# Turning logit spectra on chip with VectorE block transpositions, and a new order for the hand-over to the experts

## The chip, the cores and the metric

One Trainium2 chip (trn2), one core. The metric is device time in microseconds of one execution, the median of several. The profile and the trace are of one execution on that core. PE is the matrix engine (TensorE), PEld its weight loads, DVE is VectorE, ACT is ScalarE, POOL is GpSimd, SP only issues DMAs.

## The reference, cut to what matters

```python
X = np.fft.rfft(x, axis=1)                       # x: 8 batches x 3072 x 256
Yr = Xr @ w_r - Xi @ w_i + b_r;  Yi = Xr @ w_i + Xi @ w_r + b_i
Y  = soft_threshold(Yr, 0.01) + 1j * soft_threshold(Yi, 0.01)
x  = np.fft.irfft(Y, n=3072, axis=1).reshape(24576, 256)
logits = x @ phi                                  # 32 slots
d = softmax(logits, over tokens);  slot_input = d.T @ x
slot_out[e] = relu(slot_input[e] @ w1[e]) @ w2[e] # 8 experts, 4 slots each, 1024 wide
c = softmax(logits, over slots);   x = c @ slot_out
out = mish(x @ w_in) @ w_out                      # 2048 wide
```

All arrays are float32. The token softmax runs over all 24576 tokens, so nothing of the experts can start before the last batch's logits have been weighed.

## The kernel before, in words

The transform of length 3072 is done as 128 x 24. For each batch `stage1` multiplies by the 128-point matrix `f1`, the result goes to memory and comes back with the frequencies in other places (`load_b`), and for each of 32 blocks (four per batch, eight frequency pairs each) `stage2` multiplies by twiddled 24-point matrices. `xh` and `xl` are the rounded value and its rest: for each of six PSUM tiles of a block ACT copies `xh` (L230) and DVE subtracts `xl` (L231), one pair after the other. `linear` is the complex product, in groups of six matmuls `l` (three groups for each half of the features, here called a, b and c by their weights), followed on DVE and ACT by `k`, `p`, `cl` and on POOL by `yt`. `ytrans` transposes `yt` to `y` for the slot sums.

The logits need no inverse transform of the 256 features: `project` (`pp`) applies phi to the spectrum first, giving 32 slots, DVE transposes that (`phat`), `inv1` (`iu`) does the 24-point part of the inverse, and `inv2` (`lps`) the 128-point part for a whole batch. Between `inv1` and `inv2` the axes have to be exchanged. Before, `inv1` transposes 32x32 blocks on DVE into `u` (L295), stores them to the memory tensor `udr` in four pieces per block (L300), and `c_load` reads the batch back as `v` (L314). Then come the maximum over tokens (`smax1`: `rm`; `smax2`: `mt`, `mb`), the exponential `dx` (`smax3`), the softmax over slots (`csoft1`, `csoft2`, `ctrans`, stored to `c_d`), the forward transform of the weights `dx` (`fwd1`: `dps`, copied to `dm`, stored to `ddr` and read back as `dd` by `d_load`; `fwd2`: `dt`; `dturn`: `tn`), the slot sums with `y` (`slots`: `sps`) and the weight sums (`dsum`, `dsum2`: `rd`, `dsp`). A running maximum rescales sums of earlier batches.

The order of the work on every engine is that in which the pieces are issued: each piece is put in a list with a position (`at`), block k at about k, and the list is sorted. The table `PA` gives offsets for all batches and `TAIL` the positions for the last ones; there `NK` is 32, the number of blocks. Engines run their own instructions in that order, and SP its DMAs. `warm` issues small products that nothing reads.

After the last block comes the hand-over: the remaining `y`, the last batch's logits, weights and slot sums, the weight sum, and `sip`, which makes the slot inputs `sit`. Then the experts (`hp`, `htp`, `so`, `sop`), the mixed matrix `mp`, and the FFN over 24576 tokens (`h`, `g`, `o`, from L785), which fills the rest. Expert weights are loaded into room that the loop's pools leave (`right.close`, position "rc"; tiles `w1t` and `w2t`), and, once `sit` is made and the left pools are closed, `raw` (three more `w2`), `win`, `ctt` and `wof`.

Of the kernel before, what the change touches and what calls it, by code (L numbers as in the profile page):

```python
# [24 lines left out]
FF = 2048  # L25
LAM = 0.01
TINY2 = float(np.array([897 << 20], np.int32).view(np.float32)[0].astype(np.float64) ** 2)


def constants():  # L30
# [38 lines left out]
def body(ctx, tc, x, w_r, w_i, b_r, b_i, phi, w1, w2, w_in, w_out, cbig, ct, out, dbg=None, stop=False):  # L69
# [53 lines left out]
    x_t, b_t, xh_t, xl_t, yt_t, y_t, pt_t, k1_t = {}, {}, {}, {}, {}, {}, {}, {}  # L123
    sdr, udr, ddr, ch, a_t = {}, {}, {}, {}, {}
    XC = 512
# [185 lines left out]

    def c_load(b):
        v = cp.tile([128, N2, NS], F32, tag="v", name="v")
        nc.sync.dma_start(out=v, in_=udr[b].rearrange("q (r n) s -> (q r) n s", r=4))  # L314
        ch[b] = v

    def inv2(b):
        v = ch[b]
        lg = cp.tile([128, 6, 4, NS], F32, tag="lg", name="lg")
        for i in range(2):  # L320
            ps = psum([128, 12, NS], "lps")
            nc.tensor.matmul(ps, lhsT=f1t, rhs=v[:, 12 * i:12 * i + 12], start=True, stop=True)
            nc.scalar.activation(out=lg[:, :, 2 * i:2 * i + 2].rearrange("p i j s -> p j i s"), in_=ps.rearrange("p (j i) s -> p j i s", j=2),
                                 func=AF.Copy, scale=1.0 / 1536.0)
        ch[b] = lg

    def smax1(b):
        lg = ch[b]
        rm = sm.tile([128, 2, NS], F32, tag="rm", bufs=1, name="rm")
        for i in range(2):  # L330
            nc.vector.tensor_reduce(rm[:, i], lg[:, :, 2 * i:2 * i + 2].rearrange("p i j s -> p s i j"), axis=AX.XY, op=ALU.max)
        rm4 = sm.tile([128, 4, NS], F32, tag="rm4", name="rm4")
        nc.vector.tensor_max(rm4, rm[:, None, 0].to_broadcast([128, 4, NS]), rm[:, None, 1].to_broadcast([128, 4, NS]))
        ch[b, 4] = rm4

    def smax2(b):
# [18 lines left out]
    def smax3(b):  # L355
        lg = ch[b]
        ps = psum([128, NS], "mb")
        nc.tensor.matmul(ps, lhsT=ones32, rhs=ch[b, 2], start=True, stop=True)
        dx = cp.tile([128, N2, NS], F32, tag="dd", name="dx")
        nc.vector.tensor_sub(dx.rearrange("p (j i) s -> p j i s", j=4), lg.rearrange("p i j s -> p j i s"),  # L360
                             ps[:, None, None, :].to_broadcast([128, 4, 6, NS]))
        nc.scalar.activation(out=dx, in_=dx, func=AF.Exp)
        ch[b, 1] = dx
# [31 lines left out]
    def fwd1(b):  # L395
        d = ch[b, 1]
        dm = cp.tile([128, N2, NS], F32, tag="v", name="dm")
        for i in range(2):
            ps = psum([128, 12, NS], "dps")
            nc.tensor.matmul(ps, lhsT=f1, rhs=d[:, 12 * i:12 * i + 12], start=True, stop=True)  # L400
            nc.scalar.activation(out=dm[:, 12 * i:12 * i + 12], in_=ps, func=AF.Copy)
        ddr[b] = dram.tile([NP, 96, NS], F32, tag="ddr", bufs=2, name="ddr")
        (nc.scalar if b == NB - 1 else nc.sync).dma_start(out=ddr[b].rearrange("q (r n) s -> (q r) n s", r=4), in_=dm)

    def d_load(b):
        dd = cp.tile([96, NP, NS], F32, tag="dd", name="dd")
        nc.sync.dma_start(out=dd, in_=ddr[b].rearrange("q p s -> p q s"))
        ch[b, 0] = dd

# [8 lines left out]
    def dsum2(b):  # L418
# [4 lines left out]
        else:  # L423
            ab = ab_t[b]
            nc.vector.tensor_scalar(d_acc, d_acc, ab[:, 0:1], None, op0=ALU.mult)
            nc.vector.scalar_tensor_tensor(d_acc, ps, ab[:, 1:2], d_acc, op0=ALU.mult, op1=ALU.add)

    def fwd2(b, g):
        dd = ch[b, 0]
        ps = psum([128, 2, 96], "dt")  # L430
        for i in range(2):
            for j in range(4):
                q = 8 * g + 2 * j + i
                nc.tensor.matmul(ps[32 * j:32 * j + 32, i], lhsT=dd[:, q, :], rhs=t_m[:, q, 0:96],
                                 start=True, stop=True, tile_position=(0, 32 * j))
        dt = cp.tile([128, 2, 96], F32, tag="pt", bufs=2, name="dtt")
        nc.scalar.activation(out=dt, in_=ps, func=AF.Copy)
        ch[b, 7, g] = dt

    def dturn(b, g):  # L440
# [4 lines left out]
        t = cp.tile([96, 2, 128], F32, tag="dh", bufs=4, name="dh")  # L445
        nc.scalar.activation(out=t, in_=ps, func=AF.Copy)
        ch[b, 5, g] = t
# [35 lines left out]
    def conv(srcd, dstd, i, step):  # L483
# [5 lines left out]
        if step == 1:  # L489
            src = cv["n"]  # L490
            cv.update(lo=src[:, :, 0].bitcast(U32), hi=src[:, :, 1])
            for t in "abc":
                cv[t] = cvp.tile([128, n], I32, tag="c" + t, name="cv" + t)
        lo, hi, a, b, c = (cv[t] for t in ("lo", "hi", "a", "b", "c"))
        if step == 1:
# [53 lines left out]
    for b in range(NB):  # L549
        f2 = pos("f2", b)  # L550
        for n, f in (("cl", c_load), ("i2", inv2), ("m1", smax1), ("m2", smax2), ("m3", smax3), ("f1", fwd1), ("c1", csoft1),
                     ("ds", dsum), ("dl", d_load), ("c2", csoft2), ("ds2", dsum2)):
            at(pos(n, b), f, b)
        for g in range(4):
            at(f2 + 0.1 * g, fwd2, b, g)
            at(f2 + 0.1 * g + 0.15, dturn, b, g)
        if b < NB - 1:
            at(pos("sl", b), slots, b)
        else:
            for g in range(4):  # L560
                at(f2 + 0.1 * g + 0.27, slots, b, (g,))
        for g in range(2):
# [85 lines left out]
class Experts:  # L648
# [37 lines left out]
    def run(self, big, psh, pso, sit, ident, sot, load_rest):  # L686
# [39 lines left out]
        for g in range(2):  # L726
# [3 lines left out]
            for h in range(2):  # L730
# [4 lines left out]

PA = dict(y=20, s1=-5.89, s1d=0.3402, lb=-1.91, s2=-1.1, s2d=0.0002, pj=1.18, yt=2.24, ytd=0.0002, cl=0.78, i2=1.17, m1=1.17, m2=1.34, m3=1.51, f1=1.84, c1=1.58, ds=1.76, dl=2.05, c2=2.57, ds2=8.73, f2=2.46, sl=3.2, rc=0.3, cx=3.24, cxd=0.0002, x0=-0.79, x1=0.05, ytl=1.05, x2=1.3, x3=2.7)


TAIL = {
# [7 lines left out]
    "warm": ((0.83, 7), (1.175, 5), (1.3, 2), (1.395, 3), (1.76, 20), (2.32, 15), (3.5, 4)),  # L747
}
# [134 lines left out]
```

## Time and profile before

| | us |
|---|---|
| median of 3 runs | 1995.45 |
| lowest, highest | 1987.47, 1995.67 |
| profiled execution: span from the first to the last instruction | 1995.2 |
| PE busy in the span | 1942.3 (97%) |
| DVE, ACT, POOL busy | 1169.1, 903.3, 195.1 |
| chain that ended last: PE, ACT, DVE | 80%, 9%, 6% |

The profiled execution's own time is not listed apart from its span; the span lies 0.25 us below the median. Busy time of PE is from matmuls that overlap, so it is read together with the idle notes of its rows: a wait is written as [us of idle <- what ended it]. A share over the whole span mixes three stages (loop, hand-over, FFN), so the rows below are by stretch.

### The profile page before, as it was taken

The numbers are of one execution on the slowest core, as the hardware profiler recorded it, in microseconds if no ns is written. First come the engines' busy times: TensorE is split into PE (matmuls) and PEld (weight loads), VectorE is DVE, ScalarE is ACT, GpSimd is POOL, SyncE is SP. The second block draws the span as 40 slices with busy tenths as digits, with TensorE's granted clock in tenths as the row PEclk, the third lists the DMA queues.
The fourth block names the chain that finished last, engine by engine and source line by source line (L and its number), as shares of the span: only waits on it lengthen the run. The fifth ranks groups of instructions, "written<-read, shape, count | busy, mean of one in ns | idle before, by whom it ended". The sixth has DMA issues, their size and how long they took to land.

```text
span 1995.2 us, 30611 instructions
## 1 busy us (share of the span) xinstructions
PE 1942.3 (97%) x12344; PEld 1623.3 (81%) x12344; DVE 1169.1 (59%) x1767; ACT 903.3 (45%) x1479; POOL 195.1 (10%) x245
## 2 busy tenths in 40 slices
PE   7899999999998999999999999999999999999999
PEld 5677787777877768888888888888888888888887
DVE  3345545556455547666666666666666666666665
ACT  2666666667665433333333333333333333333332
POOL 0332332332323100000000000000000000000000
PEclk9999998999999899999999999999999999999999
DMA  8755665566643690002002002002002002000000
GB/s 248 233 151 173 167 185 141 170 173 160 184 142 78 213 297 27 20 13 53 22 22 53 22 22 53 22 22 53 11 22 53 22 22 53 22 22 22 22 22 22
DMA packets 131150, 171.39 MB, mean 86 GB/s; under 512 B 57136, under 2 KB 96688, under 8 KB 130752
## 3 DMA queue, kind: packets, MB, share of 16 engines
q1 hardware_dynamic: 128512, 164.10, 28.0%
q0 software_dynamic: 1792, 4.76, 0.8%
q8 instruction: 97, 1.59, 0.3%
q10 hardware_dynamic: 704, 0.57, 0.1%
q14 instruction: 45, 0.37, 0.1%
HBM read 102.29 MB, written 67.11 MB: 85 GB/s over the span
## 4 chain that ended last, share of the span: by engine, by line
PE 80%; ACT 9%; DVE 6%; issue 2%; POOL 1%; DMA 1%; ACTq 0%; SPq 0%; DVEq 0%; POOLq 0%
PE o L815 54%; PE h L785 9%; PE l L250 5%; DVE xl L231 3%; PE s L222 3%; ACT xh L230 2%; PE s L193 2%; ACT cl L268 2%; ACT p L269 2%; PE sps L457 1%; ACT y L309 1%; PE tr L307 1%; POOL yt L270 1%; DVE p L262 1%; PE pp L281 1%
## 5 line engine op out<-in xcount | busy, mean ns | idle before, releaser
L815 PE MATMUL o<-whl,gh 128*128 128x512 f32 x3072 | 1082.9, 395 | 0.0
L815 PE MATMUL o<-whl,gl 128*128 128x256 f32 x3072 | 827.8, 280 | 0.0
L791 ACT ACTIVATE g<-h 128x1024 f32<-128x1024 f32 x384 | 394.3, 1027 | 746.3 <-PE h L785 733.6
L815 PEld LDWEIGHTS o<-whl,gh 128*128 128x128 f32 x3072 | 566.5, 188 | 121.5
L815 PEld LDWEIGHTS o<-whl,gl 128*128 128x128 f32 x3072 | 578.5, 188 | 31.5
L800 DVE TENSOR_TENSOR gl<-g,gh 128x1024 fp32r<-128x1024 f32 x384 | 470.2, 1224 | 28.9 <-DVE gh L796 0.9
L796 DVE CAST gh<-g 128x1024 fp32r<-128x1024 f32 x384 | 265.8, 692 | 351.1 <-ACT g L791 351.0
L785 PE MATMUL h<-ctt,mst 128*128 128x512 f32 x768 | 240.8, 395 | 0.0
L231 DVE TENSOR_TENSOR xl<-s,xh 128x432 fp32r<-128x432 f32 (+1 forms) x192 | 106.1, 558 | 153.1 <-ACT xh L230 153.1
L270 POOL TENSOR_TENSOR yt<-cl,p 128x384 f32<-128x384 f32 x124 | 126.2, 1017 | 435.1 <-ACT p L269 309.6
L222 PE MATMUL s<-tall,bt 96*128 96x144 f32 x1024 | 137.0, 294 | 8.9 <-DMA bt<-sdr 4.5
L222 PEld LDWEIGHTS s<-tall,bt 96*128 96x128 f32 x1024 | 134.9, 197 | 13.0 <-issue 12.0
L230 ACT ACTIVATE xh<-s 128x432 fp32r<-128x432 f32 (+1 forms) x192 | 90.8, 490 | 114.0 <-DVE xl L231 77.4
L785 PEld LDWEIGHTS h<-ctt,mst 128*128 128x128 f32 x768 | 121.2, 188 | 17.9 <-DVE mst L772 0.5
L262 DVE TENSOR_TENSOR p<-l,k 128x384 f32<-128x384 f32 x128 | 70.6, 553 | 91.3 <-PE l L250 58.9
L823 DVE TENSOR_TENSOR os<-o,os 128x256 f32<-128x256 f32 x192 | 76.6, 419 | 77.4 <-ACT os L822 77.4
L268 ACT ACTIVATE cl<-p,tup 128x384 f32<-128x384 f32 x124 | 76.3, 615 | 91.6 <-DVE p L262 71.4
L193 PE MATMUL s<-xc,cb 128*128 128x512 f32 x192 | 103.8, 632 | 7.8 <-DMA xc<-in_x_dram 7.8
L822 ACT ACTIVATE os<-o 128x256 f32<-128x256 f32 x192 | 73.7, 384 | 41.6 <-PE o L815 37.7
L269 ACT ACTIVATE p<-p,tlo 128x384 f32<-128x384 f32 x124 | 76.4, 616 | 4.0
L309 ACT ACTIVATE y<-tr 96x512 f32<-96x512 f32 x128 | 66.1, 592 | 14.6 <-PE tr L307 14.6
L307 PEld LDWEIGHTS tr<-cb,yt 128*96 128x96 f32 x512 | 54.0, 126 | 18.9 <-DVE xl L231 7.0
(176 smaller groups left out, 1539.7 us busy)
## 6 DMA issues: line engine op xcount, KB each, us to landing
bt<-sdr SPq DMA_DIRECT2D x32, 768.0 KB, 8.2
out_dram<-os SPq DMA_DIRECT2D x47, 512.0 KB, 2.6
xc<-in_x_dram SPq DMA_DIRECT2D x42, 512.0 KB, 5.2
sdr<-a SPq DMA_DIRECT2D x42, 512.0 KB, 3.2
ctt<-c_d SPq DMA_DIRECT2D x28, 384.0 KB, 7.1
c_d<-chl SPq DMA_DIRECT2D x16, 384.0 KB, 3.1
w1t<-in_moe_w_dram SPq DMA_DIRECT2D x6, 1024.0 KB, 6.9
w2t<-in_moe_w_dram SPq DMA_DIRECT2D x5, 1024.0 KB, 11.0
```

The costliest lines, as they stand in the source:

```text
L193: nc.tensor.matmul(ps, lhsT=f1, rhs=xs, start=True, stop=True)
L222: nc.tensor.matmul(ps[:, i], lhsT=b_t[k][:, p0 + i, h * 128:(h + 1) * 128], rhs=t_m[:, 8 * g + p0 + i, :], start=True, stop=True)
L230: nc.scalar.activation(out=xh, in_=ps, func=AF.Copy)
L231: nc.vector.tensor_sub(part(xl_t[k]), ps, xh.bitcast(F32))
L268: nc.scalar.activation(out=cl, in_=p, func=AF.Relu, bias=tup[:, ri, eh:eh + 1])
L269: nc.scalar.activation(out=p, in_=p, func=AF.Relu, scale=-1.0, bias=tlo[:, ri, eh:eh + 1])
L270: nc.gpsimd.tensor_sub(yt[:, eh, :, ri, :], cl, p)
L785: nc.tensor.matmul(ps[:, i], lhsT=mst[:, f * 128:f * 128 + 128], rhs=ct_t[b][:, 4 * m:4 * m + 4].rearrange("p n t -> p (n t)"), start=True ...
L791: nc.scalar.activation(out=g, in_=h_t.pop(p), func=AF.Mish)
L796: nc.vector.tensor_copy(gh, g)
L800: nc.vector.tensor_sub(gl, g, gh.bitcast(F32))
L815: nc.tensor.matmul(o, lhsT=a[:, i, ts], rhs=w, start=f == 0 and n == 0, stop=f == 15 and n == 1)
```

## The change

`inv1` no longer transposes and stores. ACT copies its PSUM tile into `st`, one tile per batch, laid out so that each token residue's 32 columns stand together; `sturn` then makes `v` for the batch with one DVE block transposition (two halves in the last batch). The rows of `f1.T` are permuted to match. `c_load`, `udr` and `u` go. Only in the last batch the forward part does the same: `fwd1` transposes from PSUM into `dm`, and `d_load` turns `dm` with PE transpositions (`td`) instead of store and load; there also the maximum is taken from PSUM, `dx` is made in two halves, and some copies move to DVE (`evict`). The tile `cvb` of the weight conversion goes. The position table of the hand-over is new: the last two batches' slot sums and `y` transpositions are spread between the steps, most `warm` products go, and the loads of the expert weights stand together.

```diff
     def inv1(k):
...
-        u = cp.tile([128, 2, 3, NS], F32, tag="u", bufs=2, name="u")
-        nc.vector.transpose(out=u.rearrange("p i a s -> p (i a s)"), in_=ps.rearrange("p i f -> p (i f)"))
         if g == 0:
-            udr[b] = dram.tile([NP, 96, NS], F32, tag="udr", bufs=2, name="udr")
-        for j in range(4):
-            q = 8 * g + 2 * j
-            (nc.scalar if k == NK - 1 and j > 1 else nc.sync).dma_start(out=udr[b][q:q + 2].rearrange("i (a n) s -> n i a s", n=32), in_=u[32 * j:32 * j + 32])
+            spt[b] = cp.tile([128, N2, 32], F32, tag="st", name="st")
+        nc.scalar.activation(out=spt[b].rearrange("p n (g i r) -> p g i r n", g=4, i=2)[:, g],
+                             in_=ps.rearrange("p i (r n) -> p i r n", r=4), func=AF.Copy)
...
-    def c_load(b):
-        v = cp.tile([128, N2, NS], F32, tag="v", name="v")
-        nc.sync.dma_start(out=v, in_=udr[b].rearrange("q (r n) s -> (q r) n s", r=4))
+    def sturn(b):
+        v = cp.tile([128, N2, NS], F32, tag="dd", name="v")
+        n = 2 if b == NB - 1 else 1
+        for i in range(n):
+            c = slice(N2 // n * i, N2 // n * (i + 1))
+            nc.vector.transpose(out=v[:, c].rearrange("p n s -> p (n s)"), in_=spt[b][:, c].rearrange("p n q -> p (n q)"))
         ch[b] = v
...
     def fwd1(b):
...
+            if last:
+                nc.vector.transpose(out=dm.rearrange("p q n -> p n q")[:, 12 * i:12 * i + 12], in_=ps)
+            else:
+                nc.scalar.activation(out=dm[:, 12 * i:12 * i + 12], in_=ps, func=AF.Copy)
...
     def d_load(b):
...
+        for a in range(2):
+            ps = psum([96, 4, 128], "td")
+            for c in range(4):
+                nc.tensor.transpose(ps[:, c], src[:, 4 * a + c], ident)
...
-PA = dict(... cl=0.78, i2=1.17, ...)
+PA = dict(... tu=1.0, i2=1.17, ...)
```

(The two lines on `PA` are cut; the rest of that table is the same.)

The first place is DVE in the fifth batch, between the block's `xl` subtractions and the maximum `rm` of the logits. Before, the rows were:

```order
L231 TENSOR_TENSOR xl<-s_5047,xh 128x3x3x48
L231 TENSOR_TENSOR xl<-s_5053,xh 128x2x3x48
L262 TENSOR_TENSOR p<-l,k_5068 128x384
L331 TENSOR_REDUCE rm<-lg 128x32 x2
L333 TENSOR_TENSOR rm_5095<-rm 128x128
```

and now:

```order
L234 TENSOR_TENSOR xl<-s_4923,xh 128x3x3x48
L234 TENSOR_TENSOR xl<-s_4929,xh 128x2x3x48
L317 STREAM_TRANSPOSE v<-st 128x768
L265 TENSOR_TENSOR p<-l,k_4944 128x384
L343 TENSOR_REDUCE rm<-lg 128x32 x2
L345 TENSOR_TENSOR rm_4973<-rm 128x128
```

The transposition that makes `v` stands behind the last of the six `xl`; in the other six batches it stands there too, with at most one conversion step between.

The second place is PE at the same point, now, with the waits of each instruction (the engine whose count it waits for):

```order
L253 MATMUL l<-xh,bh 128x384
L253 MATMUL l<-xl,bh 128x384
L253 MATMUL l<-xh,bl 128x384
L327 MATMUL lps<-v,cb 128x384 [waits DVE_49,PE_49]
L327 MATMUL lps<-v,cb 128x384 [waits PE_49]
L196 MATMUL s_4975<-xc,cb 128x512 [waits PE_49]
L284 MATMUL pp<-yt,ph 32x256 [waits PE_49,Pool_49]
```

Before, PE's rows stood in the same order here, and the first `lps` waited for a DMA and for the release of its PSUM tile by DVE; now it waits for DVE's transposition.

The third place is PE in the hand-over, from the last `inv1` to the forward transform of the last batch. Before:

```order
L292 MATMUL iu<-tall,phat 32x96 x8
L420 MATMUL dsp<-ones,rd_6171 128x1
L420 MATMUL dsp<-ones,rd_7070 128x1
L389 MATMUL ctps<-cb,lg 128x128 x6
L457 MATMUL sps<-y,dh 32x256 x32
L307 MATMUL tr<-cb,yt 96x128 x16
L477 MATMUL wm<-cb 128x128 x7
L322 MATMUL lps<-v,cb 128x384 x2
L307 MATMUL tr<-cb,yt 96x128 x8
L477 MATMUL wm<-cb 128x128 x5
```

and now:

```order
L295 MATMUL iu<-tall,phat 32x96 x8
L506 MATMUL sps<-y,dh 32x256 x16
L327 MATMUL lps<-v,cb 128x384 x2
L506 MATMUL sps<-y,dh 32x256 x8
L350 MATMUL mt<-cb,rm_7315 128x128
L506 MATMUL sps<-y,dh 32x256 x8
L374 MATMUL mb<-mdg,ones_107 128x32
L307 MATMUL tr<-cb,yt 96x128 x8
L421 MATMUL dps<-dx,cb 128x384 x2
L307 MATMUL tr<-cb,yt 96x128 x8
L443 MATMUL td<-cb,dm 96x128 x8
L307 MATMUL tr<-cb,yt 96x128 x4
```

The slot sums `sps` of the seventh batch and the transpositions `tr` now stand between the steps of the last batch, where `wm` stood, and the transpositions of block 29 (the two `tr` rows of eight), which free the room of the expert weights, stand on both sides of `dps`.

## Rows read from the trace of the kernel before

**Rows 1.** By stretch: us; PE, PEld, DVE, ACT, POOL busy; granted clock; DMA share; GB/s.
```profile
100.00:660.00 560.00, 532.77 (x4226) 426.23 (x4225) 305.64 (x656) 366.16 (x760) 172.11 (x213) 0.97 0.56 155
735.00:1990.00 1255.00, 1255.00 (x6917) 1083.21 (x6917) 797.57 (x965) 467.54 (x581) 0.00 (x0) 1.00 0.10 31
```

**Rows 2.** Timeline of PE, fifth batch: start us, us, instruction, [idle before <- releaser].
```profile
465.18 1.45 PE L322 MATMUL lps<-v,cb 128*128 128x384 f32 x4
...
468.51 2.19 PE L307 MATMUL tr<-cb,yt 128*96 128x128 f32 x16
471.56 0.44 PE L250 MATMUL l<-xh,ch 128*128 128x384 f32 x1 [0.87 <-ACT lg L323]
...
473.65 0.30 PE L338 MATMUL mt<-cb,rm 128*128 128x128 f32 x1 [0.77 <-DVE rm L333]
```

**Rows 3.** Timeline of DVE, fifth batch, the last subtraction of the block.
```profile
468.78 0.46 DVE L231 TENSOR_TENSOR xl<-s,xh 128x288 fp32r<-128x288 f32 x1 [0.54 <-ACT xh L230]
```

**Rows 4.** Timeline of ACT, fifth batch, the first copy of the same block.
```profile
462.99 0.51 ACT L230 ACTIVATE xh<-s 128x432 fp32r<-128x432 f32 x1
```

**Rows 5.** Timeline of PE, first and seventh batch, and a wait in the third.
```profile
138.86 1.45 PE L322 MATMUL lps<-v,cb 128*128 128x384 f32 x4
...
146.60 0.30 PE L338 MATMUL mt<-cb,rm 128*128 128x128 f32 x1 [0.76 <-DVE rm L333]
...
333.95 0.42 PE L444 MATMUL tn<-cb,dtt 128*96 128x128 f32 x2 [1.50 <-ACT dtt L437]
...
622.52 0.91 PE L322 MATMUL lps<-v,cb 128*128 128x384 f32 x2 [0.27 <-DVE xl L231]
...
632.93 0.45 PE L338 MATMUL mt<-cb,rm 128*128 128x128 f32 x1 [2.39 <-DVE rm L333]
```

**Rows 6.** Timeline of DVE, first and seventh batch, the last subtraction of the block.
```profile
141.15 0.46 DVE L231 TENSOR_TENSOR xl<-s,xh 128x288 fp32r<-128x288 f32 x1 [0.54 <-ACT xh L230]
...
627.12 0.46 DVE L231 TENSOR_TENSOR xl<-s,xh 128x288 fp32r<-128x288 f32 x1 [0.55 <-ACT xh L230]
```

**Rows 7.** Groups by shape, 100 to 660: shapes xcount | busy us, mean ns | idle before.
```profile
L295 DVE STREAM_TRANSPOSE u<-iu 128x192 f32<-128x192 f32 x28 | 10.6, 377 | 6.3 <-PE iu L292 6.2
L413 DVE TENSOR_REDUCE rd<-dx 128x32 f32<-128x768 f32 x7 | 10.5, 1494 | 0.0
...
L437 ACT ACTIVATE dtt<-dt 128x192 f32<-128x192 f32 x27 | 8.8, 325 | 1.9 <-PE dt L434 1.9
```

**Rows 8.** Busy time by stretch, columns as in the first group, around waits of PE.
```profile
326.00:346.00 20.00, 18.50 (x174) 15.24 (x172) 9.51 (x23) 12.97 (x29) 6.00 (x7) 0.91 0.75 195
461.00:481.00 20.00, 18.28 (x116) 13.57 (x115) 12.91 (x28) 13.60 (x28) 5.88 (x8) 1.00 0.53 145
626.00:642.00 16.00, 12.63 (x71) 10.04 (x71) 11.18 (x24) 9.34 (x18) 3.37 (x5) 0.79 0.07 16
```

**Rows 9.** Timeline of PE in the hand-over, from the last block to the FFN.
```profile
672.48 1.91 PE L307 MATMUL tr<-cb,yt 128*96 128x128 f32 x16
...
676.25 0.54 PE L292 MATMUL iu<-tall,phat 96*32 96x96 f32 x16 [0.64 <-DVE phat L284]
...
684.90 1.46 PE L322 MATMUL lps<-v,cb 128*128 128x384 f32 x4
...
691.65 1.56 PE L400 MATMUL dps<-dx,cb 128*128 128x384 f32 x4 [0.24 <-ACT dx L362]
...
704.56 0.87 PE L434 MATMUL dt<-tall,dd 96*32 96x96 f32 x32 [0.53 <-DMA dd<-ddr]
...
713.46 5.36 PE L697 MATMUL hp<-w1t,sit 128*32 128x512 f32 x48 [0.32 <-DVE sit L601]
...
731.54 3.70 PE L767 MATMUL mp<-win,sot 128*128 128x512 f32 x8 [0.32 <-DVE sot L732]
```

**Rows 10.** Busy time by stretch, columns as in the first group, while the weights load.
```profile
704.00:716.00 12.00, 11.05 (x173) 6.11 (x176) 0.71 (x2) 3.21 (x9) 0.00 (x0) 1.00 1.06 338
716.00:728.00 12.00, 11.65 (x152) 5.88 (x148) 3.00 (x5) 1.89 (x4) 0.00 (x0) 1.00 1.07 405
```

More of the change, by code (lines that the diff above doesn't have):

```diff
@@ L323, in inv2 @@
             nc.scalar.activation(out=lg[:, :, 2 * i:2 * i + 2].rearrange("p i j s -> p j i s"), in_=ps.rearrange("p (j i) s -> p j i s", j=2),
-                                 func=AF.Copy, scale=1.0 / 1536.0)
+                                 func=AF.Copy, scale=SC)
+            if b == NB - 1:
+                nc.vector.tensor_reduce(rm[:, i], ps.rearrange("p n s -> p s n"), axis=AX.X, op=ALU.max)
         ch[b] = lg
+        if b == NB - 1:
+            ch[b, 3] = rm
     def smax1(b):
[L328 to L331, printed above, removed]
+        if b == NB - 1:
+            rm = ch[b, 3]
+        else:
+            lg = ch[b]
+            rm = sm.tile([128, 2, NS], F32, tag="rm", bufs=1, name="rm")
+            for i in range(2):
+                nc.vector.tensor_reduce(rm[:, i], lg[:, :, 2 * i:2 * i + 2].rearrange("p i j s -> p s i j"), axis=AX.XY, op=ALU.max)
         rm4 = sm.tile([128, 4, NS], F32, tag="rm4", name="rm4")
@@ L359, in smax3 @@
         dx = cp.tile([128, N2, NS], F32, tag="dd", name="dx")
-        nc.vector.tensor_sub(dx.rearrange("p (j i) s -> p j i s", j=4), lg.rearrange("p i j s -> p j i s"),
-                             ps[:, None, None, :].to_broadcast([128, 4, 6, NS]))
-        nc.scalar.activation(out=dx, in_=dx, func=AF.Exp)
+        dv, lv = dx.rearrange("p (j i) s -> p j i s", j=4), lg.rearrange("p i j s -> p j i s")
+        n = 2 if b == NB - 1 else 1
+        w = 4 // n
+        for i in range(n):
+            c = slice(w * i, w * i + w)
+            nc.vector.tensor_sub(dv[:, c], lv[:, c], ps[:, None, None, :].to_broadcast([128, w, 6, NS]))
+            nc.scalar.activation(out=dx[:, 6 * w * i:6 * w * (i + 1)], in_=dx[:, 6 * w * i:6 * w * (i + 1)], func=AF.Exp)
         ch[b, 1] = dx
@@ L396, in fwd1 @@
         d = ch[b, 1]
-        dm = cp.tile([128, N2, NS], F32, tag="v", name="dm")
+        last = b == NB - 1
+        dm = cp.tile([128, 32, N2] if last else [128, N2, NS], F32, tag="st" if last else "chl", bufs=1 if last else 2, name="dm")
         for i in range(2):
@@ L400, in fwd1 @@
             nc.tensor.matmul(ps, lhsT=f1, rhs=d[:, 12 * i:12 * i + 12], start=True, stop=True)
-            nc.scalar.activation(out=dm[:, 12 * i:12 * i + 12], in_=ps, func=AF.Copy)
+            if last:
+                nc.vector.transpose(out=dm.rearrange("p q n -> p n q")[:, 12 * i:12 * i + 12], in_=ps)
+            else:
+                nc.scalar.activation(out=dm[:, 12 * i:12 * i + 12], in_=ps, func=AF.Copy)
+        if last:
+            ch[b, 0] = dm
+            return
         ddr[b] = dram.tile([NP, 96, NS], F32, tag="ddr", bufs=2, name="ddr")
-        (nc.scalar if b == NB - 1 else nc.sync).dma_start(out=ddr[b].rearrange("q (r n) s -> (q r) n s", r=4), in_=dm)
+        nc.sync.dma_start(out=ddr[b].rearrange("q (r n) s -> (q r) n s", r=4), in_=dm)
     def d_load(b):
-        dd = cp.tile([96, NP, NS], F32, tag="dd", name="dd")
-        nc.sync.dma_start(out=dd, in_=ddr[b].rearrange("q p s -> p q s"))
-        ch[b, 0] = dd
+        if b < NB - 1:
+            dd = cp.tile([96, NP, NS], F32, tag="dd", name="dd")
+            nc.sync.dma_start(out=dd, in_=ddr[b].rearrange("q p s -> p q s"))
+            ch[b, 0] = [dd[:, q] for q in range(NP)]
+            return
+        src = ch[b, 0].rearrange("p (c r) n -> p c (r n)", r=4)
+        ch[b, 0] = [None] * NP
+        for a in range(2):
+            ps = psum([96, 4, 128], "td")
+            for c in range(4):
+                nc.tensor.transpose(ps[:, c], src[:, 4 * a + c], ident)
+            dd = yp.tile([96, 4, 128], F32, tag="y", name="dd")
+            if a:
+                nc.vector.tensor_copy(dd, ps)
+            else:
+                nc.scalar.activation(out=dd, in_=ps, func=AF.Copy)
+            for c in range(4):
+                for g in range(4):
+                    ch[b, 0][8 * g + 4 * a + c] = dd[:, c, 32 * g:32 * g + 32]
     def dsum(b):
@@ L426, in dsum2, with evict @@
             nc.vector.scalar_tensor_tensor(d_acc, ps, ab[:, 1:2], d_acc, op0=ALU.mult, op1=ALU.add)
+    def evict(b, v, out, ps):
+        if v and b == NB - 1:
+            nc.vector.tensor_copy(out, ps)
+        else:
+            nc.scalar.activation(out=out, in_=ps, func=AF.Copy)
     def fwd2(b, g):
@@ L445, in dturn @@
         t = cp.tile([96, 2, 128], F32, tag="dh", bufs=4, name="dh")
-        nc.scalar.activation(out=t, in_=ps, func=AF.Copy)
+        evict(b, g % 2, t, ps)
         ch[b, 5, g] = t
```

49 lines of the change are left out of this document (29 added, 20 removed), and 15 rows, old and new, of the table TAIL.

## The prediction

> **What bounds the kernel now.** I read the busy time by stretches first, then TensorE's own instructions around the logit spectra, then the hand-over. From 100 to 660 us PE is busy 533 of 560 us at a granted clock of 0.97, ACT 366, DVE 306, the DMA engines 0.56; from 735 us on PE is busy 1255 of 1255 us [rows 1]. So the transform loop is PE's throughput with some 27 us of waits, the expert FFN is PE without a gap, and whatever moves the start of the FFN moves the end by as much. Between them lies the hand-over, about 672 to 735 us, where a chain of small steps and the weight loads decide. The change touches the loop and the hand-over and nothing after.
>
> **The loop: what is taken away.** Per batch four transpositions of `u` (0.377 us each on DVE) [rows 7], sixteen small stores and one load of `v`. None of them is waited for: in the fifth batch PE starts `lps` at 465.18 without an idle note [rows 2], though `v` comes through memory. DVE has 254 idle us of 560 and the DMA engines are a bit over half used [rows 1]. I take the gain in the loop as 0. What hides it is PE's own queue; if PE were not the bound, DVE's saving (4 x 0.377 less the new 0.95 below) would be 0.6 us a batch.
>
> **The loop: what is added on ACT.** 32 copies of 128x192 from PSUM. Nearest row: the copy `dtt` of the same size, 0.325 us [rows 7], so 10 us in all on an engine with 194 idle us in the stretch [rows 1]. It stands behind other copies, not ahead of the `xh` chain that PE needs. Cost 0. Dropping the buffer `cvb` makes POOL's next weight piece wait for the store of the last; 32 pieces spread over some 580 us leave 18 us for each. Cost 0.
>
> **The loop: the new wait.** This is the term that decides. `v` is now one DVE transposition of 128x768, and on DVE it stands behind all six subtractions `xl` of the block that PE has just put into PSUM, while on PE `lps` stands where it stood, behind two groups of `l`. In the fifth batch the first `xh` copy starts at 462.99 [rows 4], the six pairs run one after the other, and the last `xl` starts at 468.78 and takes 0.46: it ends at 469.24 [rows 3]. PE asked for `lps` at 465.18 [rows 2], 4.1 us earlier. The transposition is priced from `u`: 0.377 for 192 columns, so about 1 ns a column, 0.377 + 576 ns = 0.95 us. Below it could be 0.8 if the fixed part were nothing; above, a DVE pass over 768 elements in steps costs 1.49 (`rd`) [rows 7]. I take 0.95, since the row of the same operation is nearest. So `lps` starts at 469.24 + 0.95 + 0.1 = 470.3, a wait of 5.1 us.
>
> Part of that PE would have waited anyway, a little later. From `lps` to `tr` it needs 3.33 us (465.18 to 468.51), then sixteen transpositions 1.85 (1.91 with their last end [rows 9]) and the last group of `l` 1.05 (471.56 to the start of its last row, plus that row's share), 6.2 in all; it took 8.47 up to `mt` at 473.65, with waits of 0.87 and 0.77 written on the rows [rows 2]. From 470.3 the same work gives `mt` at 476.5, and by then its maximum is done (`lg` two copies after `lps`, then 1.6 of reduction: about 474.5). Net 2.8 us. All that follows on PE moves by it, as it is PE's own queue. The first batch in the same way: last `xl` ends at 141.61 [rows 6], one conversion step of 0.28 now stands between it and `v`, `lps` moves from 138.86 to 142.95, `mt` from 146.60 [rows 5] to 149.1: 2.5. The seventh: `lps` 622.52, last `xl` ends 627.58, a step of 0.41 between, `lps` at 629.05, 5.2 of work (no `s` there), `mt` from 632.93 to 634.3: 1.4 [rows 5, 6]. The four others read the same way give 2.8, 2.5, 2.5 and 2.2. **Sum over seven batches: +16.7 us**; with the transposition between 0.8 and 1.49 it is 15.6 to 20.5.
>
> **The loop: the clock.** In the stretch 461 to 481 the two waits of 0.87 and 0.77 left the clock at 1.00. In 326 to 346, with a single wait of PE of 1.5 us on `dtt`, the mean is 0.91; in 626 to 642, with 2.39 us before `mt`, 0.79 [rows 5, 8]. As the two levels are 2.4 and 1.2 GHz, a stretch of length T at mean c loses T(1 - c) of PE's work: 1.8 and 3.4 us. A wait of 4 to 5 us at `lps` is longer than either. Two of the seven batches, the third and the seventh, have a fall near `mt` already, so five are new. I take 1.8 each, the row of a single wait, since part of the slow time then lies in the wait itself: **+9 us**, between 0 (no fall) and 17 (5 x 3.4). The Trainium skill, "TensorE: Matmul & The Clock Gate", section on HAM oscillation, tells of a kernel in which PE waited once per loop iteration and was throttled again in every one. By that rule all five falls come and the chance of my second rival goes; the fifth batch, whose two short waits cost no clock, shows that not every wait does it.
>
> **The hand-over.** Steps, all on the clock of the trace. (a) `iu` to `lps`: `iu` starts at 676.25 and `lps` at 684.90 [rows 9], through stores and a load. Now `iu` comes some 0.5 later (behind `ctps` and `dsp`), its ACT copy takes 0.33, and DVE reaches the first half of `v` after two `chl` subtractions and four small steps: `lps` at about 679.2, 5.7 earlier. (b) `lps` to `dps` took 6.75; the maxima now read PSUM and the exponentials go by halves, but two `s_acc` steps (0.8) stand ahead of `dx`: 6.0, gain 0.75. (c) `dps` to `dt` took 12.9 through memory (691.65 to 704.56); now two transpositions, eight PE transpositions and two copies: about 3.9, gain 9. (d) `dt` to `hp` took 8.9 (to 713.46). Into it now fall the 1.49 of `rd`, both class-softmax passes, eight `y` copies and the last `ctps`; the `dh` copy for the first slot sum stands on ACT behind the exponential, which waits for DVE. Laid behind each other with the durations of the same instructions: 15.6, loss 6.7. `hp` at about 704.7, 8.8 earlier.
>
> Behind it stand the weights. The first expert tiles wait until the old pools are free; now the last transpositions out of these stand behind `dps`, so I let the loads begin at about 687.4. From there 12 MiB (two `w1t`, five `w2t`, three `raw`, two `win`) and 0.8 MB of `c_d` have to land before `mp`, 13.4 MB. Over 704 to 728 the DMA engines moved 338 and 405 GB/s at a full share [rows 10], 371 in the mean: 36 us, and with 1.5 to start, `mp` at 725 where it was 731.54 [rows 9]. **Gain 6.5 us**; at 338 it is 3, at 405 the chain decides (`hp` + 18.1 = 722.8) and it is 8.7. The filler products `wm` that kept PE going are nearly gone, but a slower PE here is covered by the loads up to 2 us.
>
> **Sum.** 16.7 + 9 - 6.5 = +19 us on a span of 1995.2, so 2014.4; the median of the runs lies 0.25 above the span: 2015. Its own range, from the bounds: 15.6 + 0 - 8.7 = +7 to 20.5 + 17 - 3 = +35, 2002 to 2030.
>
> **The rivals.** *Faster: the wait at `lps` costs nothing.* It needs `v` about 1.1 us ahead of PE, or PE waits of the same size in each batch that swallow it. It decides where the last `xl` ends: at or before 464.1 instead of 469.24 in the fifth batch. Then only the hand-over counts: 1989 with the loads, and at most 14 us if PE's own instructions there (27 us behind 672.5, by their sum) were the bound and the loads kept up, 1981. For it: the seventh batch swallows 5 of its 6.5 us. Against it: the six pairs took 6.25 us from 462.99, and PE reaches `lps` in less. *The waits come, the clock holds, the loads run at 405:* 16.7 - 8.7 = +8, 2003. For it: clock 1.00 in 461 to 481. *Each fall costs what the longest wait shows and the loads run at 338:* 16.7 + 17 - 3 = +31, 2026; for it the row of 626 to 642. That the trip through memory is not really removed is no rival: the stores and the load of the inverse spectra are gone from SP's queue.
>
> **How the numbers follow.** About 0.5%, 10 us, is what a measurement of this kernel can tell from no change. Forecast 0.56 and the third case 0.14 are slower by more; the second case 0.18 is within; faster 0.12, of which about 0.02 stays within. That makes slower 0.70, same 0.20, faster 0.10. The range 1996 to 2030 leaves out the better part of the first rival and the tail above.
>
> **What would show it.** In the changed profile: an idle note of 3.5 to 5.5 us on `lps` behind `v` in each of seven batches; `mt` without its own wait; PEclk under 0.95 in the stretches that follow; the loop's end some 17 to 30 us later; `lps` to `dt` in the hand-over about 10 us; DMA share near 1 from there to `mp`. I am wrong if `lps` is not waiting, if the clock stays 1.00 after it, or if `mp` comes more than 9 us earlier relative to the loop's end.

## The result and the profile after

The changed kernel takes 2022.78 us (median of 4 runs, 2020.63 to 2023.17); the kernel before took 1995.56 us on the same chip. The ratio is 1.0141, 95% interval 1.0121 to 1.0161: slower by 1.4%. Forecast were 2015 us and a range of 1996 to 2030.

In the profiled execution (span 2018.9 us) the mixed product `mp`, behind which the FFN runs without a gap, starts at 755.02 us instead of 731.54 [rows 9], 23.5 us later, and the span is 23.7 us longer. So all of the change lies ahead of `mp`. The waits of PE, summed by what it waited for from 100 to 690 us, after (engine and line that waited, what released it, us, times, longest):

```profile
PE lps L327 <- DVE v L317: 33.6, 7, 6.7
PE tn L493 <- ACT dtt L475: 7.3, 7, 1.5
PE dt L483 <- DMA dd<-ddr: 3.0, 3, 1.8
```

and the same view of the kernel before, 100 to 660 us:

```profile
PE mt L338 <- DVE rm L333: 7.0, 7, 2.4
PE tn L444 <- ACT dtt L437: 6.6, 6, 1.7
PE l L250 <- ACT lg L323: 3.6, 6, 0.9
PE dt L434 <- DVE xl L231: 2.0, 1, 2.0
PE iu L292 <- DVE phat L284: 1.4, 2, 0.8
PE lps L322 <- DVE xl L231: 1.3, 3, 0.7
```

A new wait of 33.6 us stands at the top, seven times, and the waits at `mt` and at the group `l` behind `lps` are gone: the new wait comes ahead of them and swallows them. In the fifth batch it reads so on PE, after (compare [rows 2]):

```profile
483.23 2.90 PE L327 MATMUL lps<-v,cb 128*128 128x384 f32 x4 [4.91 <-DVE v L317]
...
488.49 1.95 PE L307 MATMUL tr<-cb,yt 128*96 128x128 f32 x16
...
491.34 0.27 PE L350 MATMUL mt<-cb,rm 128*128 128x128 f32 x1
```

and on DVE, the last `xl` of the block and the transposition behind it (compare [rows 3]):

```profile
481.74 0.46 DVE L234 TENSOR_TENSOR xl<-s,xh 128x288 fp32r<-128x288 f32 x1 [0.54 <-ACT xh L233]
482.12 0.97 DVE L317 STREAM_TRANSPOSE v<-st 128x768 f32<-128x768 f32 x1
```

The transposition ends at 483.09 and PE starts at 483.23. The four `lps` rows then take 2.90 us where they took 1.45: the clock is at its lower level. By stretches of 20 us around the wait in the first, fifth and seventh batch (columns as in [rows 1]; the fifth stood at 1.00 before [rows 8]):

```profile
134.90:154.90 20.00, 15.92 (x93) 10.91 (x92) 11.18 (x22) 11.33 (x23) 4.89 (x7) 0.91 0.41 121
...
475.00:495.00 20.00, 15.09 (x92) 10.61 (x91) 10.08 (x23) 11.33 (x24) 5.09 (x7) 0.83 0.37 106
...
642.00:662.00 20.00, 13.27 (x83) 9.41 (x82) 11.42 (x24) 10.52 (x22) 4.61 (x7) 0.83 0.02 7
```

The hand-over on PE, after (compare [rows 9]):

```profile
696.63 1.30 PE L284 MATMUL pp<-yt,ph 128*32 128x256 f32 x12
...
701.57 1.56 PE L327 MATMUL lps<-v,cb 128*128 128x384 f32 x4 [0.29 <-DVE v L317]
...
708.17 1.56 PE L421 MATMUL dps<-dx,cb 128*128 128x384 f32 x4 [0.82 <-ACT dx L382]
...
712.71 1.27 PE L483 MATMUL dt<-tall,dd 96*32 96x96 f32 x32
...
730.04 3.64 PE L746 MATMUL hp<-w1t,sit 128*32 128x512 f32 x32 [0.36 <-issue]
737.13 4.32 PE L746 MATMUL hp<-w1t,sit 128*32 128x512 f32 x16 [3.44 <-ACT hs L748]
...
755.02 3.70 PE L819 MATMUL mp<-win,sot 128*128 128x512 f32 x8 [0.32 <-DVE sot L781]
```

Counted from the last `pp` (674.32 before, 696.63 after): `lps` comes at 4.9 us instead of 10.6, `dt` at 16.1 instead of 30.2, `hp` at 33.4 instead of 39.1, but `mp` at 58.4 instead of 57.2. What was won up to `hp`, 5.7 us, is lost behind it. ACT's copy of the first `hp` tile shows on what:

```profile
736.48 1.08 ACT L748 ACTIVATE hs<-hp 128x512 f32<-128x512 f32 x2 [10.29 <-DMA c_d<-chl]
```

It waits for a store to land, and the wait of SP's queue ahead of `raw`, 6.8 us, is put down to the same store. Both tiles take room of the loop's pools, and both begin when the last `c_d` store, which reads `chl`, has landed. The chain that ended last, followed back, runs through this store too:

```profile
728.49 7.89 DMA c_d<-chl
736.48 0.61 ACT hs L748
```

From `hp` to `mp` no instruction of PE waits for a load of weights. That stretch takes 24.98 us instead of 18.08: 3.44 us are the wait at `hp`, and the other 3.45 are `hp` and `htp` behind it at a granted clock of 0.50 (737 to 743). SP's queue, after:

```profile
710.68 0.89 SPq L725 DMA_DIRECT2D w1t<-in_moe_w_dram  x2
711.62 13.91 SPq L732 DMA_DIRECT2D w2t<-in_moe_w_dram  x5
726.43 3.18 SPq L413 DMA_DIRECT2D c_d<-chl  x2
736.52 2.40 SPq L732 DMA_DIRECT2D raw<-in_moe_w_dram  x3
```

The stores are issued behind seven loads of 1 MiB, the second at 728.5, and land at 736.4; only then is `raw` issued. In the kernel before they stood behind four such loads, were issued from 701.27 on, and `raw` at 713.21. Around that point (columns as in [rows 10], which they answer to):

```profile
711.00:723.00 12.00, 10.09 (x130) 6.78 (x134) 7.61 (x13) 6.50 (x13) 0.00 (x0) 0.86 0.98 338
723.00:735.00 12.00, 10.28 (x110) 5.98 (x102) 3.31 (x11) 2.67 (x6) 0.00 (x0) 1.00 1.04 339
735.00:739.00 4.00, 1.87 (x10) 0.91 (x14) 0.00 (x0) 1.08 (x2) 0.00 (x0) 0.67 0.27 77
```

The DMA engines run at a full share and then nearly stop for 4 us.

So the account by the trace is: third group of `iu` (the first one behind the start's two long waits) to last `pp` 586.77 us instead of 563.33, +23.4; last `pp` to `mp` +1.2; the start, up to the third `iu`, 1.1 shorter. Sum +23.5. The loop's part has two rows in the view by stretches, before:

```profile
110.99:674.32 563.33, 536.10 (x4271) 428.94 (x4270) 307.96 (x658) 365.66 (x761) 172.41 (x213) 0.97 0.56 157
```

and after:

```profile
109.86:696.63 586.77, 536.53 (x4270) 426.04 (x4269) 303.19 (x636) 375.57 (x790) 170.57 (x214) 0.96 0.49 141
```

PE is busy as long as before; all 23 us are idle time. The granted clock differs by 0.01 in the mean: the kernel before had falls too, in other places. Over the parts of these two stretches in which the granted clock stood at 0.50, five before and eight after (seven of them at `lps`), the view by stretches gives these sums, before and after:

```profile
sum 30.72, PE 28.47 PEld 21.34 DVE 15.80 ACT 13.68 POOL 10.79; mean PE 5.69 PEld 4.27 DVE 3.16 ACT 2.74 POOL 2.16
...
sum 44.33, PE 33.63 PEld 14.94 DVE 25.12 ACT 20.57 POOL 1.17; mean PE 4.20 PEld 1.87 DVE 3.14 ACT 2.57 POOL 0.15
```

At half the clock PE's work takes twice as long, as the `lps` rows above do, so by these sums the falls cost PE about 14.2 us before and 16.8 after, a difference of 2.6. The loop's 23.4 us are 23.0 of idle time and 2.6 of the clock, less 2.2 by which PE's remaining busy time differs.

### The profile page after: what moved, and what is told of

The parts are those of the page before. It is cut to its first block, busy times and chain, and to the rows that moved or that the text cites. A ratio compares the mean times of both kernels' runs of the same rounds, so it can differ in the third digit from the quotient of the medians.

```text
span 2018.9 us, 30218 instructions
## 1 busy us (share of the span) xinstructions
PE 1937.6 (96%) x12252; PEld 1611.1 (80%) x12252; DVE 1168.5 (58%) x1753; ACT 912.7 (45%) x1507; POOL 193.0 (10%) x245
## 4 chain that ended last, share of the span: by engine, by line
PE 82%; ACT 7%; DVE 6%; DMA 2%; issue 2%; POOL 1%; ACTq 0%; SPq 0%; DVEq 0%; POOLq 0%
PE o L867 53%; PE h L837 9%; PE l L253 6%; PE s L225 3%; PE s L196 3%; DVE xl L234 3%; ACT xh L233 2%; PE tr L307 2%; ACT cl L271 1%; ACT p L272 1%; PE pp L284 1%; PE sps L506 1%; ACT y L309 1%; PE lps L327 1%; POOL yt L273 1%
## 5 line engine op out<-in xcount | busy, mean ns | idle before, releaser
L307 PE MATMUL tr<-cb,yt 128*96 128x128 f32 x512 | 66.6, 277 | 2.4 <-DVE xl L234 1.5
```

The source lines that it names most:

```text
L307: nc.tensor.transpose(ps[:, i, eh], yt[:, eh, 2 * c + i].rearrange("p r f -> p (r f)"), ident)
```

## The experiments

What is open: is the loop's loss the place of `v` on DVE, or the added work; how much of it is the clock; and what holds the hand-over. The kernel before ran beside each group of kernels, with medians of 1995.6, 1992.0, 1995.7 and 1993.1 us, so kernels of different groups are compared by their ratios to it.

### v in front of the block's subtractions

```diff
-PA = dict(... tu=1.0, ...)
+PA = dict(... tu=0.85, ...)
```

> The transposition that makes v stands in front of the six xl of the block instead of behind them, in all seven batches; nothing else is moved. Theory A (PE's wait at lps is DVE's queue: v behind six xh/xl pairs): the seven waits of 3.9 to 6.7 us are gone or under 1 us, the end of the loop goes back by 20 to 23 us, and the time is 2000, between 1996 and 2003. Rival B (the loop is slower because of what was added, the 28 copies st of 0.5 us on ACT and the transposition of 0.97 us on DVE, wherever they stand): the transposition now delays the xl and PE waits at l instead; 5 to 10 us of the 22 stay, the time is 2005 to 2012.

Measured: 1996.55 us, 1.0025 of before (1.0016 to 1.0035), where the changed kernel has 1.0141. That is 1.16%, 23 us, for moving seven instructions. In the trace PE no longer waits at `lps` in any batch but the seventh (0.28 and 0.35 us, as before); the fifth reads as it did in the kernel before, with its two short waits back:

```profile
466.44 1.45 PE L327 MATMUL lps<-v,cb 128*128 128x384 f32 x4
...
472.83 0.44 PE L253 MATMUL l<-xh,ch 128*128 128x384 f32 x1 [0.87 <-ACT lg L328]
...
474.91 0.30 PE L350 MATMUL mt<-cb,rm 128*128 128x128 f32 x1 [0.76 <-DVE rm L345]
```

Theory A holds: the loop, third `iu` to last `pp`, takes 558.78 us, less than the 563.33 of the kernel before, so the added copies and transpositions cost PE nothing that shows there. The 0.25% that stay in the time, 5 us, go with a lower clock over the whole run, 0.987 to 0.990 in these ten runs and 0.990 to 0.994 in the 13 of the kernel before; where in the run it falls, the one profiled execution does not show.

### v in the middle

```diff
-PA = dict(... tu=1.0, ...)
+PA = dict(... tu=0.9004, ...)
```

> The same, but v stands behind three of the six xl. Theory A: from the end of the third xl to that of the sixth is 2.7 us in the fifth batch, so the raw wait at lps falls from about 4.8 to about 2 us in each batch; as 1.5 us a batch were swallowed later in the changed kernel, most of what is left costs little: the time is 2006, between 2002 and 2011. Rival B (place does not matter, the added work does): about the same as with v in front of all six, within 3 us. Rival C (any wait of 2 us costs a fall of the clock, as much as a long one): over 2012.

Measured: 2001.13 us, 1.0045 (1.0027 to 1.0062). The waits at `lps` are 1.07, 1.59, 1.50, 1.96, 2.08, 1.06 and 3.54 us, 1.8 in the mean. The fifth batch:

```profile
472.08 2.29 PE L327 MATMUL lps<-v,cb 128*128 128x384 f32 x4 [2.08 <-DVE v L317]
```

This is 4.6 us above `v` in front, outside rival B's 3 us, and far under rival C's 2012: theory A. The time follows the place: behind none 1.0025, behind three 1.0045, behind six 1.0141. It isn't proportional: 1.8 us of wait in each batch cost about 4 us in all, 4.8 us cost 23. In the changed kernel 33.6 us of new wait made 23 us of idle time; the rest, 1.5 us a batch, only took the place of waits that PE had later on.

### The wait filled with products

```diff
     at(-4.2, warm, 36)
+    for b in range(NB - 1):
+        at(pos("i2", b) - 0.001, warm, 34)
```

> The changed kernel with 34 small products that nothing reads (about 3.9 us at full clock) on PE right before lps in each of the seven batches. The wait stays, PE is busy in it. It tells the clock from the wait. Theory A: the wait itself makes up nearly all of the loop's 22 us; the falls of the clock behind lps go, each of which slowed 2.8 to 5.5 us of work to half, but two or three falls at other waits come, as in the kernel before: the time falls by 4 to 12 us, to about 2015. Rival B (the clock is a term of 9 us or more by itself): it falls by 13 to 18 us, to 2007. Rival C (the clock costs nothing, since it falls inside the wait): within 3 us of the changed kernel.

Measured: 2026.72 us, 1.0182 (1.0161 to 1.0203), slower than the changed kernel. The size was mine to get wrong: one product is two rows of PE, so that 34 took 7.75 us, and `lps` came at 488.26 in the fifth batch, 2.65 us after `v` was done. The run doesn't decide, but it shows one thing: the clock stayed up behind `lps`, and from `lps` to `mt` it took 6.08 us instead of 8.11. So it was made again with half:

```diff
+        at(pos("i2", b) - 0.001, warm, 17)
```

> As the fill with 34 products, now with 17: one product is two rows of 0.115 us in the trace, so the 34 took 7.75 us and held lps back 2.7 us after v was there; 17 take 3.9 us and end inside each wait. Theory A: the clock no longer falls behind lps, and lps to mt takes 6.1 us instead of 8.1 as it did in the first fill; some of it is given back by falls at the other waits, which the kernel before also had. The loop ends 5 to 14 us earlier than in the changed kernel, and the time is 0.7% to 1.15% above before. Rival B (falls only fill time that PE would have waited anyway): less than 3 us, over 1.25% above before.

Measured: 2008.9 us, 1.0072 (1.0050 to 1.0093): 0.69%, 14 us, below the changed kernel, with the same waits for `v` and PE kept busy in them. The fifth batch, and the stretch around it:

```profile
472.79 3.96 PE L526 MATMUL wm<-cb 128*128 128x128 f32 x34
...
477.86 1.53 PE L327 MATMUL lps<-v,cb 128*128 128x384 f32 x4 [1.11 <-DVE v L317]
...
484.03 0.27 PE L350 MATMUL mt<-cb,rm 128*128 128x128 f32 x1
```

```profile
472.00:492.00 20.00, 18.89 (x129) 14.68 (x128) 13.65 (x28) 12.48 (x25) 4.29 (x7) 1.00 0.25 78
```

Third `iu` to last `pp` takes 573.90 us instead of 586.77: without the falls of the clock behind the seven waits the changed kernel is 12.9 us shorter (net, as two falls are left elsewhere, against one). Theory A holds in its upper half. This is not 13 of the 23 us by which the changed kernel is slower than the kernel before, which loses 14.2 us to falls of its own; what filling gives there is measured below.

### The last c_d stores on ACT's queue

```diff
-        nc.sync.dma_start(out=dst, in_=hl.bitcast(F32))
+        (nc.scalar if b == NB - 1 else nc.sync).dma_start(out=dst, in_=hl.bitcast(F32))
```

> The changed kernel with the last batch's two stores c_d issued from ACT's queue instead of SP's, where they stand behind five loads of 1 MiB. Theory A (the copies hs and the loads raw wait until the store c_d has landed, since they take the room of the tile it reads, and it lands 10 us after its issue because it is behind the loads): the store lands some 5 us earlier, the wait of 3.4 us at the second group of hp goes, raw is issued 4 to 6 us earlier, and the FFN starts 4 to 6 us earlier: 2017. Rival B (the loads set the start of the mixed matrix; the DMA engines are at a full share from 711 us on anyway): the wait at hp goes, mp waits for win instead, the time falls by under 2 us.

Measured: 2017.72 us, 1.0137 (1.0118 to 1.0157): no difference from the changed kernel that its interval shows. In the trace, `mp` comes 55.1 us after the last `pp` instead of 58.4, `raw` 37.9 instead of 39.9, and the wait at the second group of `hp` is 0.54 us instead of 3.44, but PE now waits 0.71 us for `raw`. Theory A's 4 to 6 us are not there, since the store lands hardly sooner: issued at 731.90 and 733.50, it keeps ACT waiting until 740.06:

```profile
733.50 0.37 ACTq L413 DMA_DIRECT2D c_d<-chl  x1
740.06 1.08 ACT L748 ACTIVATE hs<-hp 128x512 f32<-128x512 f32 x2 [7.19 <-DMA c_d<-chl]
```

The landing comes 6.5 us after the second issue, where it was 7.9 from SP's queue (728.5 to 736.4). The Trainium skill, "DMA: Bandwidth & Descriptors", sections "Issuing engines are not separate DMA queues" and "Queues, rings and completion order", says that SP's and ACT's queues are rings of the same sixteen DMA engines, and that a DMA's count goes up only after the earlier writes of that engine, across queues. By that rule another queue buys little here; this trace agrees with it, with 1.4 us bought.

### Two loads behind the stores

```diff
-              (..., (0.69, 2, 3, "b"), (0.723, 2, 4, "b")),
+              (..., (0.7305, 2, 3, "b"), (0.7306, 2, 4, "b")),
```

> The changed kernel with two of the five w2t loads issued behind the last c_d stores instead of in front. Theory A (hs and raw wait for the landing of c_d, and that is late because of the loads ahead of it on the queue): c_d lands 3 to 4 us after its issue instead of 10, the wait of 3.4 us at the second group of hp is gone or under 1 us, raw is issued 5 to 7 us earlier, and from the last pp to mp it takes 52 to 54 us instead of 58.4. Time 1.1% to 1.2% above before. Rival B (bytes set the start of mp): the two loads are now late themselves, so waits for w2t, and mp comes 57 us or more after pp.

Measured: 2019.27 us, 1.0118 (1.0094 to 1.0143). On SP's queue:

```profile
729.46 0.88 SPq L413 DMA_DIRECT2D c_d<-chl  x2
730.43 1.75 SPq L732 DMA_DIRECT2D w2t<-in_moe_w_dram  x2
733.69 6.90 SPq L732 DMA_DIRECT2D raw<-in_moe_w_dram  x3
```

The second store goes out at 729.9 and `raw` 3.8 us later, 34.0 us after the last `pp` instead of 39.9, and `hp` runs through its 48 rows without a wait. That part of A is shown: the landing of `c_d` holds `hs` and `raw`, and the loads ahead of it make it late. But `mp` comes at 56.0, not at 52 to 54, and PE now waits further on:

```profile
749.03 0.40 PE L762 MATMUL so<-raw,ht 128*32 128x256 f32 x1 [2.10 <-DMA raw<-in_moe_w_dram]
```

The bytes that were ahead of `c_d` are now ahead of `raw`. Behind the first limit stands a second of B's kind, though it shows at `raw`, not `w2t`: these loads all begin 14 us after the last `pp`, as late as `w1t` gets its room. With the hand-over's code unchanged, `mp` came 56.6 to 58.4 us after the last `pp` in five profiled executions (the changed kernel, `v` in front and in the middle, both fills of the long wait), so the 56.0 here lies only just below what one execution can differ from the next.

### An earlier room for the weights

The base is now the kernel with `v` in front (`tu=0.85`).

```diff
-    "yt": {... -3: (0.57, 0.571, 0.59, 0.591), ...},
-    "sl": {-2: (0.505, 0.506, 0.53, 0.55), ...},
+    "yt": {... -3: (0.53, 0.531, 0.55, 0.551), ...},
+    "sl": {-2: (0.505, 0.506, 0.57, 0.59), ...},
...
-    ("ds", -1): 0.635,
+    ("ds", -1): 0.705,
```

> With v in front of the six xl; in the hand-over two further moves. The transpositions y of block 29, which hold the room of the expert weights, change places with the last two groups of slot sums of the seventh batch, so the loads can start 4 to 5 us earlier and two s_acc steps (0.8 us on DVE) are off the path to dx; and rd (1.7 us on DVE) goes behind the softmax over slots. If the chain and the start of the loads both set mp: hp comes 31 us after the last pp instead of 33.4, mp 50 to 53 us after it instead of 56.6 with v in front alone, and the time is 0.0% to 0.2% below before. If the landing of c_d alone sets it (softmax and store no earlier): mp gains under 2 us and the time stays 0.1% to 0.2% above before.

Measured: 1993.72 us, 0.9996 (0.9982 to 1.0011): the same as before. The hand-over did what was expected, counted from the last `pp` at 674.50: `w1t` at 9.3 instead of 14.0, `hp` at 30.9, `mp` at 51.8.

```profile
683.77 0.89 SPq L725 DMA_DIRECT2D w1t<-in_moe_w_dram  x2
...
701.79 0.88 SPq L413 DMA_DIRECT2D c_d<-chl  x2
709.44 2.38 SPq L732 DMA_DIRECT2D raw<-in_moe_w_dram  x3
```

```profile
726.34 1.12 PE L819 MATMUL mp<-win,sot 128*128 128x512 f32 x2 [0.32 <-DVE sot L781]
```

The same with two loads behind the stores (the edit is that of the section on them):

> The same, and two w2t loads behind the c_d stores. If c_d's place in the queue still matters although the loads now start earlier: mp 48 to 51 us after the last pp, time 0.2% to 0.35% below before. If the queue is empty by the time c_d is issued: the same as the kernel without it, or up to 2 us slower, since the DMA engines pause in front of c_d.

Measured: 1994.25 us, 0.9994 (0.9979 to 1.0009), and `mp` at 53.3 us, not 48 to 51: the second case, up to 2 us slower, with `so` waiting 2.05 us for `raw`. In the time, which load stands first no longer matters here.

### Short waits filled, in both kernels

Both kernels gain 4 to 5 us of hand-over in the trace, against `mp` at 57.2 in the kernel before, and show little of it in the time. Their loops point to a reason: third `iu` to last `pp` is 558.78 us in the execution of `v` in front alone, 564.85 in that of the kernel above, with the same code there, at a granted clock of 0.99 and 0.97. So the falls of the clock differ from one execution to the next (two in the loop of the first, six in that of the second), and they come behind short waits too. This fills the loop's remaining waits:

```diff
+    for b in range(NB - 1):
+        at(pos("m2", b) - 0.001, warm, 10 if b == NB - 2 else 3)
+        at(pos("f2", b) + 0.149, warm, 5)
+    at(pos("f2", NB - 2) - 0.001, warm, 8)
```

once on the kernel with the earlier room:

> The kernel with v in front of the xl and the two moves in the hand-over, and small products that nothing reads in the loop's remaining waits of PE: 3 (0.7 us) before mt, 10 (2.3 us) in the seventh batch, 5 (1.2 us) before the first tn of each batch, 8 (1.8 us) before the first dt of the seventh. Theory A (short waits bring the clock down too, and its falls behind them cost some 13 us in this loop and in that of the kernel before): at most two falls are left in the loop, it is 6 to 11 us shorter, and the time is 0.25% to 0.5% below before. Rival B (the falls only hide in later waits, or the products take as much as they give): within 0.1% of before.

and once on the kernel before:

> The kernel before with the same small products at the same places, and nothing else. Theory A: its five falls in the loop, which slowed 29 us of work to half, go for the most part: 0.25% to 0.5% below before, so that the loop on chip and through memory stand side by side again, with the hand-over as the only difference. Rival B: within 0.1% of before.

Measured: 1986.53 us, 0.9965 (0.9951 to 0.9979), and 1988.77 us, 0.9980 (0.9963 to 0.9998). The loop of the first,

```profile
109.62:666.56 556.94, 541.14 (x4413) 437.18 (x4412) 303.39 (x636) 373.80 (x790) 171.21 (x213) 1.00 0.52 148
```

and of the second:

```profile
112.60:668.20 555.60, 540.31 (x4413) 437.16 (x4412) 307.44 (x658) 365.37 (x761) 172.44 (x213) 1.00 0.57 159
```

Both stand at 1.00. The first beats both kernels, by 0.35% and about 1.7%. The second gains 0.2%, less than the 0.25 to 0.5% expected of it; its profiled loop is 7.7 us shorter than that of the profile before. The five falls there cost 14.2 us, but the products (19.1 us) and the idle time that is left (15.3) are 7.2 us more than the 27.2 of idle time that they replace, so half is given back, as rival B had it in part. Side by side the loops take 556.9 and 555.6 us: on chip or through memory, PE's loop differs by 1.3 us in these two executions. The trip through memory is then not free either:

```profile
383.30 0.88 PE L322 MATMUL lps<-v,cb 128*128 128x384 f32 x2 [1.32 <-DMA v<-udr]
```

In two batches of the second (1.32 and 0.47 us) `lps` waits for `v` to come back. By the medians the first is 2.2 us ahead, where its hand-over in the trace is 5.1 us shorter; the rest is not explained.

## Why the prediction was right

**The wait.** The step that was to decide did: `v` behind six `xl`, the waits of the first, fifth and seventh batch follow from the prediction as 4.1, 5.1 and 6.5 us and measured 4.08, 4.91 and 6.73; the four others, of which it gives only the net price, measured 4.42, 4.55, 5.02 and 3.90. The transposition took 0.97 us, forecast 0.95; its slope of 1 ns a column stands in none of the rows cited, and the run bears it out. The net price was forecast at 16.7 us. Read directly, it is the 23.0 us of idle time less the 2.2 of busy time: 20.8. The two loops with filled waits, 573.9 us and 555.6 in the kernel before, give 18.3; but the first still has two falls of 4.7 us, and in the second the products are 7.2 us longer than what they fill, which brings it to 20.8 as well. So the wait was sized 4 us too low, just above the top of its own bounds (20.5). The raw waits were right; what was off is the part of them that PE would have waited later anyway, 12.8 of 33.6 us, and which of the later waits gave less than forecast stays open. `v` moved ahead and to the middle shows that place, and not work, is the cause.

**The clock.** Forecast +9 us, as five new falls at 1.8 each beside those that were there. Net it is 2.6. The seven falls at `lps` held 30.2 us of PE's work and so cost 15.1, 2.2 each: the price was near; the count against the kernel before was not. I had seen two falls there, in the third and seventh batch, worth 5.2 us by [rows 8], and left them in place. That loop has five, worth 14.2 us, and but for one at its end none stands in the changed kernel: when PE waits at `lps`, the waits at `mt` are gone and with them falls of their own. The Trainium skill, "TensorE: Matmul & The Clock Gate", section on HAM oscillation, tells of a loop that waits once per iteration and whose PE is throttled again in every one. This trace agrees for waits of 3.9 to 6.7 us, seven of seven stretches of 20 us at 0.83 to 0.91. It didn't lead me to look for the falls behind waits of 0.7 to 2.4 us, which the kernel before had.

**The hand-over.** Forecast -6.5 us, measured +1.2 (-0.7 with the same hand-over code and `v` in front): this step failed, by 7.7 us. The chain went as written for the first steps: `lps` 5.6 us earlier, counted from the last `pp` (forecast 5.7), `dps` to `dt` 8.4 less (9); `lps` to `dps` gained 0.2 instead of 0.75, and `dt` to `hp` lost 8.4 instead of 6.7, so `hp` came 5.7 us earlier, not 8.8. That is 3.1 of the 7.7 us. The rest is the sentence on the loads, "371 in the mean: 36 us, and with 1.5 to start, `mp` at 725": it lets the last load set `mp`, 20.3 us behind `hp`, and it took 24.98. The loads began about when I said (14.0 us after `pp`, forecast 13.1), and moved 338 and 339 GB/s, my lower bound, but PE waited for none of them. It waited 3.44 us at `hp` for ACT's copy `hs`, which waited for the `c_d` stores to land behind seven loads, and lost 3.45 more to the clock behind that wait, where I had a slower PE covered by the loads. `raw` waited for the same stores, and the DMA engines stood nearly still for 4 us (0.27 at 735 to 739, where I had expected a share near 1 up to `mp`). The order on SP's queue was in front of me; that the stores' landing frees the room of what comes next was not in my sum. The loads are the next limit: once the landing is earlier, `so` waits 0.5 to 2.1 us for `raw`.

**The sum.** 20.8 + 2.6 + 1.2, less the 1.1 of the start, is 23.5. Forecast was 19: the clock was 6.4 us too high, the wait 4.1 and the hand-over 7.7 too low, and they partly cancelled. The direction and the deciding wait were right; that the sum came within 5 us is in part luck. The copies `st`, forecast at 0.325 us, took 0.50; their output is permuted, which no run tested as the cause. They stayed covered. The rival that the wait is absorbed needed `v` before PE asks, which is the kernel with `v` in front: 1.0025, where its price of 1981 to 1989 us is 0.993 to 0.997 of before. The hand-over's gain, 0.7 us instead of 6.5 or more, was missing, and the 5 us of the lower clock came on top.

## What to carry to other kernels

An instruction that replaces a trip through memory takes a place in an in-order queue, and that place is part of its price: here 0.97 us of DVE work per batch, seven times, cost 23 us more behind six other instructions than in front of them. Price a wait of PE together with the fall of the clock behind it, and count the falls that are already there; products that nothing reads, no longer than the wait, are a cheap test and here the cheapest gain; where they were longer than the short waits, about half of it went back. Before a store is put behind large loads, ask whose room it frees when it lands.

## What the runs showed of the hardware that was not expected

The kernel before varies with its clock: in the 13 runs beside the first four kernels, those with a mean granted clock of 0.994 took 1988.7 to 1989.4 us, those at 0.990 took 1992.2 to 1994.8. With the short waits filled in the kernel with the earlier room, the clock is 0.994 to 0.998 and 12 runs lie between 1985.3 and 1990.2 us; in the kernel before, eleven of 12 lie between 1985.1 and 1991.4 at 0.995 to 0.998, and one took 1999.6 at 0.992. The same short wait brings the clock down in some executions and not in others: the 1.50 us at `tn` in the third batch stand in a stretch of 20 us at 0.91 in the kernel before and in the one with the earlier room, and at 1.00 with `v` in front alone, with PE busy 18.50 us in all three.
